# Two table products joined into one VectorE operation, and the whole work list and PSUM pairing written anew, in a kernel of windowed attention beside an S4 convolution

## The chip, the cores and the metric

The kernel runs on one core of one Trainium2 chip. The metric is the device time of one execution in microseconds (us). Before the change three runs took 783.17, 783.67 and 787.14 us; their median, 783.67 us, is the time before. A profile of one execution shows what each engine did: TensorE (PE, with its weight loads as PEld), VectorE (DVE), ScalarE (ACT), GpSimd (POOL) and SyncE (SP, which only issues DMAs here).

## The reference

Two independent layers work on 2048 positions and 576 channels; their outputs stand side by side.

```
A:  qkv = x @ wqkv                       32 heads of 18 channels
    scores = q k^T / sqrt(18), kept where 0 <= i - j < 256
    out_A = softmax(scores) v @ wo
B:  logdA = exp(log_dt) * A              576 channels x 128 complex states
    K[d,l] = Re sum_n C * exp(logdA * l) * exp(log_dt) * B
    y = irfft(rfft(u) * rfft(K)) + u * Dskip
```

## The kernel before, in words

**Layer A.** `proj` makes q, k and v for four blocks of 512 positions. A projection block is 14 matmuls (L204) in three pieces of 5, 5 and 4; its result goes from PSUM through ACT (L450) and DVE (L453) for q and k, or through ACT alone (L442) for v, and is stored to DRAM. The v rows of the first block come earlier, in `vfirst`, from unscaled data (matmuls L398 and L403, ACT copies L405), while the scales of x and w are being found by `amax` (DVE, L192); scaled copies then are made by ACT (L371, L382) and DVE (L372, L383, L385). `smax` finds the largest score of each row: one piece is 8 matmuls (L906 with L914 or L917) and one DVE reduction (L940). `scores` multiplies q and k again (L982, L995), and ACT takes the exponential (L1000); `pv` multiplies by v (L1020); `norm` divides (DVE, POOL and ACT, L1046 to L1063); `wo` applies the output matrix (L204 again, into PSUM pairs).

**Layer B.** The convolution kernel K comes from tables. The 576 channels are 18 quads of 32, each of two half groups of 16 channels: 36 half groups. Per half group: phases on PE (L505), folded into one turn by ACT (L511) and DVE (L514, L515), sines on ACT (L556, L557), a growth factor m on PE with its exponential on ACT (L527, left in PSUM), and on DVE the four products of `t_q` (L601 to L604) that make the table Q. Per quad: factors `mab`, `fa`, sines `tr` (L561, L562), six POOL operations (L567 to L577), and per half group two POOL products (L586) with a DVE sum (L592). From Q and the sums, `t_taps` (64 matmuls, L615) makes the taps of K, ACT moves them (L621), and `t_dft` (L631, L635) transforms a quad. Then come u's first transform (L493), spectra (L718), products (L734, L740), inverse transforms (L752, L815) and output.

**What sets the order.** Every stream of work is a generator, and each step of it (a piece) issues the instructions of one engine or posts an evacuation for later. A string for each of four stages ("front", "tables", "first", "rest") lists the pieces in the order in which they are emitted, one letter a stream, a digit for a posted evacuation: G phases and factors, M growth factor, N sines and the POOL factors, R products and their sum, X taps and transform, P projections, V the first v rows, U u's transform, s row maxima, a scores, v the product with v, w output matrix, and so on. Each engine runs its own instructions in the order of emission; semaphores hold it where data are missing. SP and POOL issue their DMAs in the same order. The streams' pieces are the same whatever the string says; only the order differs.

**PSUM.** Nearly all matmuls outside the projection write into one of three pairs of PSUM banks, `ring0` to `ring2`, each a single buffer. Which pair a step gets is read from a second string, `SLOTS`, a digit per request. A step that gets a pair must wait until the previous user's result has been evacuated.

```
    def slot(self):
        return self.p["ring" + next(self.slots)].tile([128, 2, 512], F32, name="ring")
```

Profile lines of the kernel after stand one lower than those of the kernel before up to `t_q`, where L601 becomes L600, and L603 is gone.

## Time and profile before

| | before |
|---|---|
| runs | 783.17, 783.67, 787.14 us (median 783.67) |
| profiled execution, span | 784.5 us |
| mean granted TensorE clock | 0.963 of full |
| PE busy | 693.0 us (88%) |
| DVE busy | 588.2 us (75%), 779 instructions |
| ACT busy | 534.3 us (68%) |
| POOL busy | 417.3 us (53%) |
| DMA | 150.67 MB |

The span runs from the first to the last instruction of the profiled execution, here 784.5 us, 0.8 us above the median of the runs. Busy time is a sum over the whole program; the stages have different limits, and the time slices of each stage tell which engine stands idle there and for what. The first scaled projection starts at 42.4 us, the first taps at 78.0, the first row maxima at 359.95, the last transform of the tables at 382.98, the last product with v ends at 740.6.

### The profile page before, as it was taken

The page shows a single profiled execution, that of the slowest core. Times are in us where ns is not written, and L with a number is a line of the kernel's source. Part 1 is how long each engine was busy: PE and PEld are TensorE (multiplying, and loading weights), DVE is VectorE, ACT ScalarE, POOL GpSimd, SP SyncE. Part 2 cuts the span into 40 slices and gives each one's busy share as a digit, 9 for nine tenths or more (in the row PEclk, how much of TensorE's full clock was granted, in tenths as well). Part 3 has the DMA queues.
Part 4 walks back from the last instruction along what each step waited for, and adds up shares of the span by engine and source line. Part 5 has one row for each costly group of instructions (what it writes and reads, how often), then busy time and mean ns, then how long its engine had stood idle before and what let it go on. Part 6 is the DMA issues. An engine that isn't in the chain of part 4 may idle for free.

```text
span 784.5 us, 29499 instructions
## 1 busy us (share of the span) xinstructions
PE 693.0 (88%) x12956; PEld 410.8 (52%) x12956; DVE 588.2 (75%) x779; ACT 534.3 (68%) x709; POOL 417.3 (53%) x309
## 2 busy tenths in 40 slices
PE   3786878998989989997789999989989998999997
PEld 2532444565545654665544555544555554557775
DVE  5998789998998897988777888876888586852100
ACT  2369577787887777773458677775877876786622
POOL 2245867987688666866007574451553444546120
PEclk9979799999999999996999999998999999899999
DMA  8998055738247537889578777676866786555786
GB/s 309 342 215 204 7 133 149 159 83 216 51 120 182 133 70 175 230 183 277 113 238 279 247 240 231 207 243 166 245 185 203 240 256 207 170 163 159 205 258 187
DMA packets 215904, 150.67 MB, mean 192 GB/s; under 512 B 103530, under 2 KB 195818, under 8 KB 215520
## 3 DMA queue, kind: packets, MB, share of 16 engines
q1 hardware_dynamic: 214160, 146.28, 66.0%
q0 software_dynamic: 1616, 2.52, 1.1%
q8 instruction: 101, 1.65, 0.8%
q14 instruction: 27, 0.22, 0.1%
HBM read 83.50 MB, written 65.11 MB: 189 GB/s over the span
## 4 chain that ended last, share of the span: by engine, by line
PE 55%; DVE 17%; ACT 15%; issue 6%; DMA 4%; SPq 1%; POOL 0%; ACTq 0%; DVEq 0%
PE po L1020 9%; PE pp L204 9%; PE ring L204 7%; PE ring L906 5%; DVE m L940 5%; PE ring L752 4%; PE ring L982 4%; PE ring L615 4%; PE ring L718 4%; PE ring L505 2%; DMA wraw<-in_wr_dram 2%; DVE amx L192 2%; PE ring L815 2%; ACT raw L1000 2%; DVE wl L372 2%
## 5 line engine op out<-in xcount | busy, mean ns | idle before, releaser
L940 DVE TENSOR_REDUCE m<-ring 128x2 f32<-128x640 f32 (+4 forms) x256 | 190.8, 779 | 66.0 <-PE ring L914 58.2
L586 POOL TENSOR_TENSOR m<-A,tr 128x1024 f32<-128x1024 f32 x72 | 141.5, 1983 | 52.6 <-DVE m L592 43.5
L1000 ACT ACTIVATE P<-ring,esc 128x1024 f32<-128x1024 f32 (+2 forms) x86 | 90.0, 1060 | 37.1 <-PE ring L995 32.7
L1000 ACT ACTIVATE raw<-ring,esc 128x1024 f32<-128x1024 f32 (+2 forms) x74 | 77.2, 1061 | 19.4 <-PE ring L995 18.8
L734 POOL TENSOR_TENSOR t<-X 128x768 f32<-128x768 f32 x24 | 46.7, 1944 | 76.1 <-ACT X L726 75.6
L1063 POOL TENSOR_TENSOR oh<-osb,oh 128x1024 f16<-128x1024 f32 x16 | 34.1, 2133 | 59.5 <-ACT oh L1059 42.9
L914 PE MATMUL ring<-sm,idb 64*64 64x128 bf16 x896 | 56.1, 224 | 3.3 <-issue 3.1
L204 PE MATMUL pp<-xh,wh 128*128 128x512 f16 x180 | 48.1, 397 | 10.0 <-DVE qst L453 5.0
L204 PEld LDWEIGHTS <-wh 128*128 128x128 f16 x324 | 30.7, 99 | 49.1 <-issue 11.7
L615 PE MATMUL ring<-Q,m 128*32 128x64 f32 x2304 | 42.9, 231 | 12.8 <-ACT fa L511 4.1
L1055 POOL TENSOR_TENSOR osb<-osb,T 128x1024 f32<-128x1024 f32 x16 | 38.6, 2410 | 25.8 <-DVE T L1050 23.8
L592 DVE TENSOR_TENSOR m<-m,m 128x1024 f32<-128x1024 f32 x36 | 51.6, 1432 | 0.7 <-POOL m L586 0.6
L615 PEld LDWEIGHTS ring<-Q,m 128*32 128x32 f32 x2304 | 36.9, 117 | 27.2 <-ACT mab L547 5.5
L906 PEld LDWEIGHTS <-raw 54*64 54x64 f16 x704 | 28.6, 108 | 41.1 <-issue 37.7
L740 POOL TENSOR_TENSOR Y<-t,t 128x384 f32<-128x384 f32 x24 | 24.7, 1029 | 46.1 <-DVE t L734 33.8
L906 PE MATMUL ring<-K,raw 54*64 54x320 f16 (+4 forms) x576 | 44.8, 308 | 4.5 <-ACT raw L1000 0.8
L204 PE MATMUL pp<-xh,wl 128*128 128x512 f16 x180 | 48.0, 400 | 0.6 <-DVE wl L372 0.6
L567 POOL TENSOR_TENSOR tr<-tr,mab 128x768 f32<-128x768 f32 x18 | 33.3, 1850 | 28.4 <-ACT tr L562 28.4
L726 ACT ACTIVATE X<-ring 128x768 f32<-128x768 f32 x48 | 36.7, 812 | 14.3 <-PE ring L718 8.1
L995 PE MATMUL ring<-tm,idb 64*64 64x256 bf16 (+2 forms) x640 | 45.0, 257 | 0.0
L982 PEld LDWEIGHTS <-K 55*64 55x64 f16 x1280 | 28.8, 108 | 26.7 <-issue 22.7
L752 PE MATMUL ring<-Y,i 32*64 32x192 f32 x768 | 38.7, 336 | 3.3 <-issue 2.3
(171 smaller groups left out, 1725.1 us busy)
## 6 DMA issues: line engine op xcount, KB each, us to landing
gk<-kst SPq DMA_DIRECT2D x36, 256.0 KB
gx<-ust SPq DMA_DIRECT2D x16, 576.0 KB
xk<-gx SPq DMA_DIRECT2D x24, 384.0 KB
xk<-gk SPq DMA_DIRECT2D x24, 384.0 KB
h<-ho SPq DMA_DIRECT2D x48, 192.0 KB
hp<-h SPq DMA_DIRECT2D x24, 384.0 KB
K<-kz SPq DMA_DIRECT2D x14, 512.0 KB
raw<-qz SPq DMA_DIRECT2D x11, 512.0 KB
```

The source lines that it names most:

```text
L204: self.nc.tensor.matmul(ps, u, v, start=(i == 0), stop=(i == len(ops) - 1))
L586: tt(m[part], A[:, ch, a0:a0 + 8].unsqueeze(3).to_broadcast(sh), tr[:, ch, part, 0:8].unsqueeze(2).to_broadcast(sh), op=OP.mult)
L592: self.nc.vector.tensor_tensor(m[0], m[0], m[1], op=OP.add)
L615: nc.tensor.matmul(kp[32 * st:32 * st + 32, j, :], m[:, ch, 32 * term:32 * term + 32], Q[:, ch, term, :], start=(term == 0), stop=(term == ...
L734: mul(ts[i], X[:, :, :, :192].rearrange("p i s j -> p s i j"), X[:, i, :, 192:].unsqueeze(2).to_broadcast(sh), op=OP.mult)
L752: nc.tensor.matmul(ps[64 * (b % 2):64 * (b % 2) + 64, b // 2, 192 * s:192 * s + 192], self.i1[32 * b:32 * b + 32, t, o:o + 64], Y[32 * b:3 ...
L906: nc.tensor.matmul(ps[z:z + 64, b, :n], d["Q"][rr, 2 * b + pp, 64 * qb:64 * qb + 64], d["K"][rr, 2 * b + pp, k0:k1], start=True, stop=Fals ...
L914: nc.tensor.matmul(out, self.idb[rr], self.sm[rr], start=False, stop=True, skip_group_check=True)
L940: self.nc.vector.tensor_reduce(out, x, axis=AX.X, op=OP.max)
L982: nc.tensor.matmul(ps[z:z + 64, b, off:off + w], d["K"][rr, 2 * b + pp, kc:kc + 64], d["Q"][rr, 2 * b + pp, q0:q0 + w], start=(k == 0), st ...
L1000: nc.scalar.activation(P[:, :, lo:hi], ps[:, :, lo:hi], AF.Exp, scale=self.esc)
L1020: nc.tensor.matmul(po[32 * p:32 * p + 32, z, q0:q0 + w], V[64 * z:64 * z + 64, kb * 76 + 19 * p:kb * 76 + 19 * p + 32], P[p % 2][64 * z:64 ...
```

## The change

Two of the four products of `t_q` read halves of the same sine table f (sine and cosine side by side), multiply by the same 512 values of m, and write neighbouring parts of Q. They become one `tensor_tensor` over 128x1024 elements that reads f with the two halves reversed and m twice by a broadcast. The other two products stay. Over 36 half groups that is 36 DVE instructions fewer, 743 instead of 779. The order strings of all four stages and the string of PSUM pairs are written anew; the pieces in them are otherwise the same ones, and the counts of every other instruction are unchanged, the ACT table loads too.

```diff
 PLAN = {
     "front":
-        "AAAVCACAAAAAVAVVV1CV1CAVAVAAVCAV1ACCVCACCVVV1VV1CVCACBBPABV1CCPV1BV1CPCPP1PVP2PP4CPAPP1PP2BPCP1P4BVP"
-        "CP",
+        "BAAAAAAAAAAVAAACACCCACACVVV1V1VVVV1ACACCCCCCBBBV1CACVVVPAV1BVCCV1VVCV1V1CVVBCPPPPP1",
     "tables":
...
-        "2U2G1RXPP1M1UNP4X1P5PXPGUX1PU1X2PG5X4P5GU4P2MRPU4G2MPPX4G5PP5U2XPG6PG6U4RP6M1PMNXP6GPPMRP4PGNRPRX5P5"
...
-        "5M1P4G6P6RsP5P6NU4sX2P6sU4sRMs2ss2ssX5ss2X4ssZs2s2sss2s2s2Zs2ZX1Ns2ss2sXs2s2X1ss2Rss2XZs2s",
...
+        "XX5P1RP6X2RP4PPMUU2P4P2P1U1XNRX1UP2MUM1U4PU1PPX4U2X4GG1GPMPPP5G2G5GG5G6G6P5XMX1XX4M1U4PX5RRX2MXX1sss"
+        "2s2PRssss2s2ssPs2s2s2ss2PX4X4Nssss2s2Ps2PP5MPM1NX4RRsss2PPP5XX1U4PZs2ZZPMssP6P6s2ss2s2PP5MP5P6RPXPM1"
+        "MRX5XX1X2P4P4Pss6sss2s2X4X4s4ss2sss2s2sss2s2RP5PPPP5sss2Xs2ss2X1XX5X2sss2P6",
...
@@ -598,9 +597,9 @@
         sn, cs = (f[:, i].rearrange("p (c m) -> p c m", m=32) for i in range(2))
         m = self.mg.pop(c)
         Q = self.Q[c] = self.p["Qp"].tile([128, HC, 2, 64], F32, name="Q")
-        tt(Q[:, :, 0, 32:64], cs, m[:, :, 32:64], op=OP.mult)
+        tt(Q[:, :, :, 32:64], f.rearrange("p i (c m) -> p c i m", m=32)[:, :, ::-1],
+           m[:, :, 32:64].unsqueeze(2).to_broadcast([128, HC, 2, 32]), op=OP.mult)
         tt(Q[:, :, 0, 0:32], cs[:, :, ::-1], m[:, :, 0:32], op=OP.mult)
-        tt(Q[:, :, 1, 32:64], sn, m[:, :, 32:64], op=OP.mult)
         nc.vector.scalar_tensor_tensor(Q[:, :, 1, 0:32], sn[:, :, ::-1], -1.0, m[:, :, 0:32],
                                        op0=OP.mult, op1=OP.mult)
```

Three places show what moves.

At the end of the tables, on DVE: before, the last products and sums of the tables stand among the first row maxima (L940), 16 of which come in one row.

```order
L592 TENSOR_TENSOR m_4410<-m_4410,m_4411 128x1024
L601 TENSOR_TENSOR Q<-fr,ring 128x16x32
L602 TENSOR_TENSOR Q<-fr,ring 128x16x32
L603 TENSOR_TENSOR Q<-fr,ring 128x16x32
L604 SCALAR_TENSOR_TENSOR Q<-fr,ring 128x16x32
L940 TENSOR_REDUCE m<-ring 128x2 x16
L926 TENSOR_SCALAR m_4705<-ring 32x128
L647 COPY kst<-ring 128x2x32x8
L940 TENSOR_REDUCE m<-ring 128x2 x2
```

```order
L600 TENSOR_TENSOR Q<-fr,ring 128x32x32
L602 TENSOR_TENSOR Q<-fr,ring 128x16x32
L603 SCALAR_TENSOR_TENSOR Q<-fr,ring 128x16x32
L939 TENSOR_REDUCE m<-ring 128x2 x11
L591 TENSOR_TENSOR m_4300<-m_4300,m_4301 128x1024
L939 TENSOR_REDUCE m<-ring 128x2 x2
L600 TENSOR_TENSOR Q<-fr,ring 128x32x32
L602 TENSOR_TENSOR Q<-fr,ring 128x16x32
L603 SCALAR_TENSOR_TENSOR Q<-fr,ring 128x16x32
L939 TENSOR_REDUCE m<-ring 128x2 x3
```

After, three rows stand where four stood (L600 is the joined product), and the row maxima come in groups of 11, 2 and 3 with a sum and three products between them.

At the same place on ACT: before, the last evacuation of a projection (L442, the v rows `vst`) precedes the last sines of the tables.

```order
L442 ACTIVATE vst_150<-pp,vsc 128x16x18
L511 ACTIVATE fr<-ring 128x512
L527 ACTIVATE ring<-ring 128x1024
L442 ACTIVATE vst_150<-pp,vsc 128x16x18
L556 ACT_TABLE_LOAD
L556 ACTIVATE fr<-fr 128x512
L557 ACTIVATE fr<-fr,halfpi 128x512
L556 ACTIVATE fr<-fr 128x512
L557 ACTIVATE fr<-fr,halfpi 128x512
L561 ACTIVATE tr<-fa 128x32x12
L562 ACTIVATE tr<-fa,halfpi 128x32x12
```

```order
L441 ACTIVATE vst_148<-pp,vsc 128x16x18
L526 ACT_TABLE_LOAD
L526 ACTIVATE ring<-ring 128x1024
L441 ACTIVATE vst_148<-pp,vsc 128x16x18
L620 ACTIVATE Kq<-ring 128x256
L441 ACTIVATE vst_149<-pp,vsc 128x16x18 x2
L526 ACTIVATE ring<-ring 128x1024
L646 COPY kst<-ring 128x2x32x8
L620 ACTIVATE Kq<-ring 128x256
L441 ACTIVATE vst_150<-pp,vsc 128x16x18 x2
L620 ACTIVATE Kq<-ring 128x256
L646 COPY kst<-ring 128x2x32x8
```

After, six evacuations of v rows (L441) stand behind the last sines, among the taps' copies. By the order strings no projection piece stands behind the first row maximum before, and 17 do after.

In the front, on ACT: before, the scaled copies of x and w (L382, L371) stand after all but the last two copies of the first v rows (L405).

```order
L318 ACTIVATE dt<-dt 128x576
L405 ACTIVATE vst_149<-pp 128x16x18
L382 ACTIVATE xh<-raw,xr 128x5x256 x2
L371 ACTIVATE wh<-wraw,wr 128x5x288
L405 ACTIVATE vst_150<-pp 128x16x18 x2
L371 ACTIVATE wh<-wraw,wr 128x5x288 x2
L450 ACTIVATE qst<-pp 128x512
```

```order
L317 ACTIVATE dt<-dt 128x576
L404 ACTIVATE vst_148<-pp 128x16x18
L381 ACTIVATE xh<-raw,xr 128x5x256 x2
L370 ACTIVATE wh<-wraw,wr 128x5x288
L404 ACTIVATE vst_149<-pp 128x16x18
L370 ACTIVATE wh<-wraw,wr 128x5x288 x2
L404 ACTIVATE vst_149<-pp 128x16x18
L370 ACTIVATE wh<-wraw,wr 128x5x288
L404 ACTIVATE vst_150<-pp 128x16x18 x2
L370 ACTIVATE wh<-wraw,wr 128x5x288 x2
L449 ACTIVATE qst<-pp 128x512
```

After, four copies of v rows (L404) stand between and behind the scaled copies, and the first evacuation of a scaled projection (L449) comes behind all six pieces of w.

More of the change, by code (lines that the diff above doesn't have):

```diff
@@ L104 @@
+        "MRX5XX1X2P4P4Pss6sss2s2X4X4s4ss2sss2s2sss2s2RP5PPPP5sss2Xs2ss2X1XX5X2sss2P6",
     "first":
[L105 to L106 removed]
+        "saa1s2ss2s2ss2aass2a1a1vsss6s2ssss2s2sas2s2ss2sss2a1vaaa1s2a1ss2vsaa1s2sasvs2a1X4X4aas2",
     "rest":
[L108 to L109 removed]
```

86 lines of the change are left out of this document (42 added, 44 removed).

## The prediction

> **What bounds the kernel now.** I read the page's totals first, then the time slices cut at the stage borders, then the DVE groups, then the timeline at three places.
>
> ```profile
> span 784.5 us, 29499 instructions
> PE 693.0 (88%) x12956; PEld 410.8 (52%) x12956; DVE 588.2 (75%) x779; ACT 534.3 (68%) x709; POOL 417.3 (53%) x309
> ...
> 20.00:40.00 20.00, 15.96 (x60) 10.06 (x60) 18.68 (x29) 6.52 (x12) 5.39 (x10) 0.93 0.88 330
> 40.00:60.00 20.00, 15.54 (x62) 6.48 (x63) 19.92 (x17) 13.26 (x16) 7.60 (x4) 0.82 0.96 219
> 60.00:100.00 40.00, 30.15 (x247) 14.57 (x247) 32.55 (x47) 30.96 (x49) 29.41 (x25) 0.83 0.46 109
> 100.00:220.00 120.00, 106.97 (x1537) 62.15 (x1536) 108.27 (x147) 95.91 (x152) 92.17 (x70) 0.99 0.54 128
> 220.00:340.00 120.00, 111.40 (x1492) 66.35 (x1490) 105.50 (x146) 90.92 (x147) 87.82 (x69) 1.00 0.64 158
> 340.00:358.00 18.00, 15.30 (x263) 10.83 (x267) 14.66 (x19) 14.79 (x26) 12.30 (x11) 1.00 0.84 193
> 358.00:370.00 12.00, 9.28 (x220) 6.74 (x213) 10.65 (x19) 2.24 (x6) 8.32 (x10) 0.50 0.97 293
> 370.00:382.00 12.00, 9.07 (x239) 6.87 (x235) 9.89 (x17) 5.71 (x7) 3.89 (x2) 0.79 0.56 122
> 382.00:420.00 38.00, 31.56 (x894) 17.84 (x882) 26.32 (x43) 22.21 (x29) 7.55 (x6) 1.00 0.71 213
> 420.00:740.00 320.00, 301.40 (x7651) 175.94 (x7648) 228.31 (x292) 234.88 (x253) 151.95 (x96) 0.98 0.71 214
> 740.00:784.50 44.50, 39.79 (x329) 28.66 (x312) 2.85 (x3) 12.46 (x16) 6.60 (x3) 1.00 0.70 218
> ```
>
> Columns of the slices: length, busy us of PE, PEld, DVE, ACT and POOL with instructions, granted clock, DMA share, GB/s. PE is busy 693.0 of 784.5 us, so 91.5 us of idling and what a low clock stretches is all that a new order can win, since the same matmuls run. After 420 PE is full (301.4 of 320): little to win. From 20 to 60 DVE is full (38.6 of 40). From 100 to 340 PE (218.4 of 240) and DVE (213.8 of 240) are both near their limit, each waiting now and then for the other. From 358 to 382 both idle a little (PE 5.65 of 24, DVE 3.46) and the clock stands at 0.50 for half of it. From 382 to 420 PE idles 6.44 us.
>
> The costs on DVE, by groups (columns: instructions, shapes, count, busy us, mean ns, idle before and for what):
>
> ```profile
> L940 DVE TENSOR_REDUCE m<-ring 128x2 f32<-128x640 f32 x224 | 176.4, 821 | 60.0 <-PE ring L914 58.2
> L592 DVE TENSOR_TENSOR m<-m,m 128x1024 f32<-128x1024 f32 x36 | 51.6, 1432 | 0.7 <-POOL m L586 0.6
> L515 DVE TENSOR_SCALAR fr<-fr 128x512 int32<-128x512 int32 x36 | 35.7, 992 | 1.2
> L601 DVE TENSOR_TENSOR Q<-fr,ring 128x512 f32<-128x512 f32 x36 | 24.5, 680 | 7.6 <-ACT ring L527 4.9 <-PE ring L615 2.0 <-ACT fr L557 0.7
> L302 DVE TENSOR_TENSOR rre<-nA_re,hre 96x768 f32<-96x768 f32 x1 | 0.9, 945 | 0.0
> ```
>
> **Part 1, the joined product.** One half group in the timeline of DVE (start, duration), and one sum of 1024 elements beside it:
>
> ```profile
> 206.25 0.68 DVE L601 TENSOR_TENSOR Q<-fr,ring 128x512 f32<-128x512 f32 x1
> ...
> 207.44 0.68 DVE L603 TENSOR_TENSOR Q<-fr,ring 128x512 f32<-128x512 f32 x1
> ...
> 213.19 1.21 DVE L592 TENSOR_TENSOR m<-m,m 128x1024 f32<-128x1024 f32 x1
> 214.32 0.68 DVE L647 COPY kst<-ring 128x512 f32<-128x512 f32 x1
> ```
>
> The products overlap: 0.68 us long, but two of them take 207.44 - 206.25 = 1.19 us of DVE's time. The trace has no product of 1024 elements with an operand in PSUM. The nearest row, L592, has both operands in SBUF and in this undisturbed case takes 214.32 - 213.19 = 1.13 us from start to start. So the join saves 1.19 - 1.13 = 0.06 us, 36 times: 2.3 us. Upper bound: the joined product reads m once and costs no more than one of 512 (0.60): 36 x 0.59 = 21 us. Lower bound: it takes the mean of L592, 1.43, which is stretched by POOL's products beside it: 36 x (1.19 - 1.43) = -8.6 us. I take 2.3, since the elements written are as many as before and the undisturbed row is of that size; an operand in PSUM speaks against the stretched one, as L601 shows (680 ns mean, against 0.68 undisturbed).
>
> [...]
>
> What of the 2.3 us reaches the end? DVE is a bound from 100 to 340, where 28 of the 36 lie, but it shares that with PE. I count half here, 1.2 us.
>
> **Part 2, the front.** The first scaled projection waits for DVE's maxima, then ACT's copies:
>
> ```profile
> 10.75 3.15 DVE L192 TENSOR_REDUCE amx<-wraw 128x1 f32<-128x2880 f32 x1 [4.17 <-DMA wraw<-in_wr_dram]
> ...
> 35.15 1.48 DVE L192 TENSOR_REDUCE amx<-raw 128x1 f32<-128x1280 f32 x1
> ...
> 37.16 0.56 POOL L252 DMA_DIRECT2D c_ca<-in_c_ca_dram  x1
> ...
> 38.08 2.61 ACT L382 ACTIVATE xh<-raw,xr 128x1280 f16<-128x1280 f32 x2 [2.56 <-DVE xr L188]
> ...
> 40.60 1.48 ACT L371 ACTIVATE wh<-wraw,wr 128x1440 f16<-128x1440 f32 x1
> ...
> 42.42 2.29 PE L204 MATMUL pp<-xh,wh 128*128 128x512 f16 x5 [2.76 <-ACT vst L405]
> ...
> 78.01 1.29 PE L615 MATMUL ring<-Q,m 128*32 128x64 f32 x40 [4.12 <-ACT fa L511]
> ```
>
> In the new order the four operations of L302 (945 ns each, 3.8 us) come ahead of the first maximum, into DVE's 4.17 us gap before 10.75, where they cost nothing; before, they stand between maxima. Against that, POOL issues the four table constants (0.74 MB by their shapes) at the start, and not from 37.16 on, after the scales: at the 330 GB/s of the slice 20 to 40 that is 2.2 us ahead of the last blocks of x, if DMA has no slack (it is 0.88 busy there, so 0 to 2.2). At the worst of that 1.6 us remain, which I take. The copies of v (L405) move behind ACT's scaled copies, so that the first projection starts some 4 to 5 us later (two copies of x, 2.61 us, and one of w, 1.48, stand ahead of the buffers it needs). I price this at nothing: before the first taps fewer projection pieces stand in the front (5 against 12), and DVE, not PE, carries the path to the taps at 78; PE only waits there (4.12 us). Without that cover it costs the 5 us, and part 3 has the pieces to fill less. Bounds for the front: -5 to +4.
>
> **Part 3, the end of the tables.** Before, nothing but row maxima and the last three half groups are left for PE:
>
> ```profile
> 357.42 1.57 PE L615 MATMUL ring<-Q,m 128*32 128x64 f32 x64 [1.10 <-DVE kst L647]
> ...
> 359.95 0.27 PE L906 MATMUL ring<-raw 54*64 54x64 f16 x4 [0.95 <-ACT kst L647]
> ...
> 361.51 7.83 DVE L940 TENSOR_REDUCE m<-ring 128x2 f32<-128x128 f32 x14
> ...
> 369.94 0.38 ACT L621 ACTIVATE Kq<-ring 128x256 f32<-128x256 f32 x1 [9.76 <-PE ring L615]
> ```
>
> Each maximum is a matmul group, a wait, and a DVE reduction of up to 0.82 us, through three PSUM pairs: DVE sets the pace (14 in 7.83 us), the matmuls are too thin, the clock falls, and the taps behind them come late (ACT waits 9.76 us for them). In the new order 17 projection pieces stand among these maxima, which before are all done by then. Such a piece is five matmuls of 128x288:
>
> ```profile
> L204 PE MATMUL pp<-wh,xh 128*128 128x288 f16 x120 | 18.7, 286 | 1.9 <-ACT vst L442 0.9 <-DVE qst L453 0.9
> 740.54 0.79 PE L204 MATMUL ring<-woh,oh 128*128 128x288 f16 x5
> 741.16 0.78 PE L204 MATMUL ring<-wol,oh 128*128 128x288 f16 x5
> ```
>
> From start to start five such take 0.62 us (the other rows of the output matrix), so 17 pieces are about 10 us of PE work that needs no DVE (L442 evacuates them on ACT, which has only 2.24 us to do in 358 to 370). They leave the stage from 100 to 340, where PE runs at 91%, and go where PE idles 5.65 us and is slow. What they win cannot exceed what DVE has free, since DVE's work up to the last transform of the tables stays: 3.46 us between 358 and 382 and 3.34 between 340 and 358. I take the first, 3.5 us, and 1.0 for the 0.50 clock: in those 12 us 9.28 are busy, at full clock at most half, 4.6, would be saved, but DVE paces most of that. Bounds: 0 (the idle time only moves) to 5.65 + 4.6 = 10.
>
> **Part 4, behind the tables.** From 382 to 420 PE idles 6.44 us and DVE 11.68, on chains of maximum, score and exponential that wait for each other. The new order starts more maxima early: the tables hold 29 of them where 17 stood, and the "first" stage is 18 pieces shorter. Twelve maxima are 12 x 0.82 = 9.8 us of DVE work moved ahead; they fill holes there, and here PE's wait shrinks. I take a quarter of the 6.44, 1.6 us; bounds -3 to 5. From 420 to 740 PE has 18.6 us idle; the same pieces in another order give no row that prices them, so 0, with -6 to +6 (a third either way).
>
> At the end one row of SP's queue, the load of the last output block:
>
> ```profile
> 760.65 0.93 SPq L1129 DMA_DIRECT2D oh<-od  x1
> ```
>
> After the last product with v, the final normalization, its DMA round trip and the last output block stay a chain; in SP's order an output of the convolution now comes ahead of that block's loads. That is one DMA issue, which takes up to 0.93 us here (this row); half of it, -0.4.
>
> **The sum.** 1.2 + 1.6 + 3.5 + 1.0 + 1.6 + 0 - 0.4 = 8.5 us, which I round to 8, from 784.5 to 776.5 us of the profile. The median of the runs shown, 783.67, lies 0.8 below that execution, so the prediction is 775.7 us.
>
> **The rivals.** (1) *The idle time only moves.* For it: up to 382 DVE has the same work but for 2.3 us, and both PE and DVE are near full from 100 to 340, so that pieces pulled out of the tables leave holes there. Then only the join and half of the front count: 1.2 + 0.8 = 2 us, 781.7. Against it: the projection pieces are independent of DVE's chain in the tail.
>
> (2) *Slower: POOL's products stretch DVE.* The fold in the view of its line (least, median, most ns):
>
> ```profile
> L515 DVE TENSOR_SCALAR fr<-fr x36: 426/854/2252, 60.2 to 355.0; 128x512 int32<-128x512 int32 x36
> ```
>
> DVE operations with both sides in SBUF are long whenever POOL works beside them: L592 means 1432 ns against 1.21 undisturbed, L515 992 where the fastest takes 426, so 36 x (0.22 + 0.56) = 28 us are lost now. In the new order M, X and G pieces come in clusters; if the folds and sums fall behind POOL's products a third more often, 9 us are added to DVE, which carries the tables; with the late first projection (5 us, part 2) taken as hidden this gives 784.5 + 9 - 2.3 (join) - 0.8, about 790. It decides as soon as the stretch grows by more than the 8 us won, some 30%. Against it: POOL's work is unchanged and the products stay 72.
>
> (3) *The clock stays up.* If the 17 pieces keep PE above the point where the clock falls, all of the 4.6 us in 358 to 370 comes back, not 1.0: 772. For it: the slices before 358 and after 382, with denser PE work, stand at 1.00.
>
> [...]
>
> **How the numbers follow.** My forecast, 773 to 779.5, has 0.45; the clock case, 767 to 773, 0.15; idle time that only moves, 780 to 786, 0.22; the slower case, 787.6 to 796, 0.18. A measurement of this kernel tells no less than about 0.5%, 3.9 us, from no change: faster means under 779.8, slower over 787.6. So faster 0.60, same 0.22, slower 0.18. The range from 767 to 787.6 leaves out the slower case and a few hundredths below; the likeliest case's own range is 773 to 779.5.
>
> **What would show it.** The join: a group of 36 at 128x1024 near 1.2 us mean, 1.13 from start to start where nothing waits; 1.4 would show the lower bound. The front: first taps at about 76.4, not 78.0; over 80 shows the late copies of v. The tail: projection matmuls among the first maxima, the last transform of the tables at about 376, not 383, and clock above 0.50 there. Rival 1: the last transform at 381 or later with PE idle higher in 100 to 340. Rival 2: L591 (the sum) over 1.5 us and L514 (the fold) over 1.1 us mean, DVE's busy time over 595 us. The prediction is wrong if the stage after 420, which I took as even, gains or loses more than 6 us.

## The result

The changed kernel is slower: 814.15 us median (810.06 to 815.98) against 783.42 for the kernel before on the same chip, a ratio of 1.038 with the interval [1.033, 1.043]. The profiled execution took 812.7 us where the one of before took 784.5. The forecast was 775.7, with the range ending at 787.6. A few executions of a kernel run more than 1.5% above its fastest one; the medians and ratios below leave these out.

The totals of the page after:

```profile
span 812.7 us, 29455 instructions
...
PE 697.1 (86%) x12956; PEld 410.1 (50%) x12956; DVE 602.1 (74%) x743; ACT 534.7 (66%) x709; POOL 424.9 (52%) x309
```

PE does the same 12956 matmuls in nearly the same busy time (697.1 against 693.0): 24.1 of the 28.2 us are idling. DVE has 36 instructions fewer and yet is busy 13.9 us longer.

The slices of the prediction, cut at the same times (length, busy us of PE, PEld, DVE, ACT, POOL with instructions, granted clock, DMA share, GB/s):

```profile
20.00:40.00 20.00, 12.49 (x45) 8.24 (x44) 15.17 (x14) 2.83 (x6) 1.04 (x2) 0.90 1.01 387
...
100.00:220.00 120.00, 104.72 (x1445) 60.98 (x1444) 107.54 (x125) 91.04 (x143) 90.65 (x70) 0.96 0.55 134
220.00:340.00 120.00, 104.62 (x1417) 60.31 (x1421) 106.77 (x124) 88.79 (x144) 89.53 (x70) 0.99 0.56 136
...
358.00:370.00 12.00, 10.00 (x266) 6.86 (x264) 11.68 (x20) 8.41 (x15) 5.29 (x4) 1.00 0.73 166
...
420.00:740.00 320.00, 292.14 (x7495) 166.99 (x7495) 233.23 (x296) 228.75 (x249) 151.41 (x97) 0.98 0.68 207
```

Three losses and one gain stand in these rows. From 20 to 40 DVE is no longer full (15.17 of 20 where it was 18.68): it waits, beside a full DMA (1.01, 0.88 before). From 100 to 340 PE does less in the same time (209.3 us of 240, 218.4 before) while DVE is as full as it was (214.3, 213.8 before). From 420 to 740 PE has lost 9.3 us. And the thin stage from 358 to 370 stands at full clock with DVE at 11.68 of 12: this is the one place where the change does what was forecast.

Fixed times shift as the kernels part, so the rest of this text cuts by landmarks in the work instead: the first taps matmul, the 15th and the 18th (last) transform of the tables, the first spectrum, the end of the last product with v. Length of each stage in us, by the start of these matmuls in the traces; e1 is the kernel before with the joined product alone, whose execution is closest to the medians of the old order. (A run's time is 1.7 to 1.8 us above its span, 814.44 for 812.7 and in e1 780.72 for 778.9; so the profiled execution of before, 784.5, took some 786.2 us, 2.6 above its median, where the prediction set span and median side by side and took 0.8.)

```
                                   before     e1   after
start to first taps                  78.0   77.8    82.6
tables, to the 15th transform       256.5  253.6   264.1
end of the tables, 15th to 18th      48.5   49.7    44.1
18th transform to first spectrum     23.6   23.5    29.4
first spectrum to last v            334.1  329.4   340.8
last v to the end                    43.9   44.9    51.7
all                                 784.5  778.9   812.7
```

Against e1 the change loses 4.8 in the front, 10.4 in the tables, wins 5.7 at their end, and then loses 5.9, 11.4 and 6.8. The work between two landmarks isn't quite the same, since the order moves matmuls past them. PE's idle time in each stage, and the matmuls that start in it (e1 has the matmuls of before):

```
                                 idle, us: before     e1   after     matmuls: before  after
start to first taps                          28.2   28.0    31.8                 188    180
tables, to the 15th transform                25.2   24.9    34.5                3170   3136
end of the tables, 15th to 18th               8.6    8.5     4.3                 789    815
18th transform to first spectrum              4.8    4.5     6.1                 490    586
first spectrum to last v                     20.0   18.3    28.2                8016   7944
last v to the end                             4.7    5.5    10.7                 303    295
all                                          91.5   89.7   115.6               12956  12956
```

So most of the 5.9 us behind the 18th transform is work: 96 matmuls more stand ahead of the first spectrum, and 72 fewer behind it. Over the end of the tables the granted clock is 1.00 where it was 0.82, and DVE is busy 42.4 us of 44.1 where it was 40.6 of 48.5. Five stages lose and one wins: no single wait does it, so the experiments take them apart.

### The profile page after: what moved, and what is told of

Same layout as the page of the kernel before. It is cut to its first block, busy times and chain, and to the rows that moved or that the text cites. A ratio compares the mean times of both kernels' runs of the same rounds, so it can differ in the third digit from the quotient of the medians.

```text
span 812.7 us, 29455 instructions
## 1 busy us (share of the span) xinstructions
PE 697.1 (86%) x12956; PEld 410.1 (50%) x12956; DVE 602.1 (74%) x743; ACT 534.7 (66%) x709; POOL 424.9 (52%) x309
## 3 DMA queue, kind: packets, MB, share of 16 engines
q8 instruction: 101, 1.65, 0.9%
## 4 chain that ended last, share of the span: by engine, by line
PE 38%; DVE 26%; DMA 16%; SPq 7%; issue 6%; ACT 6%; POOL 0%; ACTq 0%; DVEq 0%; POOLq 0%
PE po L1019 6%; PE pp L203 6%; PE ring L203 6%; DVE m L939 4%; PE ring L905 4%; DMA hp<-h 4%; DMA K<-kz 4%; PE ring L981 3%; DVE m L591 3%; DMA wraw<-in_wr_dram 3%; DVE Q L600 3%; PE ring L751 3%; PE ring L717 2%; PE ring L492 2%; DVE Q L602 2%
## 5 line engine op out<-in xcount | busy, mean ns | idle before, releaser
L585 POOL TENSOR_TENSOR m<-A,tr 128x1024 f32<-128x1024 f32 x72 | 144.0, 2017 | 60.2 <-DVE m L591 51.5
L591 DVE TENSOR_TENSOR m<-m,m 128x1024 f32<-128x1024 f32 x36 | 60.8, 1689 | 4.1 <-POOL m L585 4.1
L739 POOL TENSOR_TENSOR Y<-t,t 128x384 f32<-128x384 f32 x24 | 24.1, 1003 | 59.5 <-DVE t L733 36.7
L614 PE MATMUL ring<-Q,m 128*32 128x64 f32 x2304 | 39.9, 222 | 14.1 <-DVE m L591 4.9
L600 DVE TENSOR_TENSOR Q<-fr,ring 128x1024 f32<-128x1024 f32 x36 | 43.6, 1212 | 6.6 <-ACT ring L526 6.4
L614 PEld LDWEIGHTS ring<-Q,m 128*32 128x32 f32 x2304 | 34.5, 111 | 25.9 <-issue 6.3
L397 PE MATMUL pp<-wraw,raw 128*128 128x288 f32 x64 | 23.1, 528 | 26.9 <-DMA raw<-in_xr_dram 16.5
```

The source lines that it names most:

```text
L585: tt(m[part], A[:, ch, a0:a0 + 8].unsqueeze(3).to_broadcast(sh), tr[:, ch, part, 0:8].unsqueeze(2).to_broadcast(sh), op=OP.mult)
L591: self.nc.vector.tensor_tensor(m[0], m[0], m[1], op=OP.add)
L600: tt(Q[:, :, :, 32:64], f.rearrange("p i (c m) -> p c i m", m=32)[:, :, ::-1], m[:, :, 32:64].unsqueeze(2).to_broadcast([128, HC, 2, 32]), ...
L614: nc.tensor.matmul(kp[32 * st:32 * st + 32, j, :], m[:, ch, 32 * term:32 * term + 32], Q[:, ch, term, :], start=(term == 0), stop=(term == ...
```

## Experiments

Theory A at the start was that the joined product is harmless and the order costs the time; the rival, that the join costs it.

### The join alone, and the order alone (e1, e2)

e1 is the kernel before with this edit, e2 the changed kernel without it:

```diff
-        tt(Q[:, :, 0, 32:64], cs, m[:, :, 32:64], op=OP.mult)
+        tt(Q[:, :, :, 32:64], f.rearrange("p i (c m) -> p c i m", m=32)[:, :, ::-1],
+           m[:, :, 32:64].unsqueeze(2).to_broadcast([128, HC, 2, 32]), op=OP.mult)
...
-        tt(Q[:, :, 1, 32:64], sn, m[:, :, 32:64], op=OP.mult)
```

> The kernel before with the joined product alone, order and PSUM pairs as they were. Theory A (the loss is all in the order; the join is worth its rows, 0.06 us of DVE 36 times, and DVE shares the limit with PE): 781 to 784 us. Rival B (the join itself costs: one operation of 1.2 us holds DVE longer where others wait behind it, or reads PSUM slowly): over 787 us.

> The kernel after with the four separate products, so the new order alone. Theory A: the whole loss stays and the join's 1 to 2 us are missing: 815 to 818 us. Rival B (the join is the cause): under 795 us.

e1 measured 782.69, ratio 1.003 [0.999, 1.006]; e2 measured 813.99, ratio 1.042 [1.034, 1.049]. The join moves the time by nothing that can be measured, and the order with its pairs carries the whole loss. In e1 the joined product has this row among the groups of DVE:

```profile
L601 DVE TENSOR_TENSOR Q<-fr,ring 128x1024 f32<-128x1024 f32 x36 | 43.7, 1214 | 6.2 <-ACT ring L527 4.9 <-ACT fr L557 0.7 <-PE ring L615 0.4
```

### Which stages (e3, e4)

e3 takes the old order through the stages "tables" and "first" and the new one for "rest"; e4 the reverse. Both have the joined product, and each part its own PSUM pairs. Only the tables of order change:

```diff
 PLAN = {
-    "front": (new)    "tables": (new)    "first": (new)
+    "front": (old)    "tables": (old)    "first": (old)
     "rest": (new)
```

> Joined product; the pieces up to the end of the tables in the old order, all that is left in the new order. In the trace of after, the last transform of the tables ends 7.7 us late, the first spectrum starts 13.6 us late, the last product with v ends 20 us late and the program 28 us. Theory A (each stretch loses its own share): 783 - 1 + 28 - 10 to 13 = 797 to 800 us. Rival B (the later stages only inherit the late start of the tables): 782 to 786 us. Rival C (only the later stages lose): 808 us and more.

> Joined product; the pieces up to the end of the tables in the new order, all that is left in the old order. Theory A: 783 + 8 to 13 = 791 to 796 us. Rival B (the loss starts in the tables and grows by itself): 808 us and more. Rival C (only the later stages lose): 782 to 786 us.

e3: 806.22, ratio 1.032 [1.025, 1.039]. e4: 792.93, ratio 1.015 [1.008, 1.023]. The new order of the rest costs 23 to 25 us, that of front and tables 9 to 11, together 32 to 36, a little more than the 31 to be explained. By the landmarks e3 takes 342.7 us from the first spectrum to the last v and 50.6 to the end; e4 takes 328.0 and 44.6, as the old order does. The stretch from the 18th transform to the first spectrum is 28.3 us in e3, behind the old tables, and 25.8 in e4, behind the new ones: most of its growth, too, comes with the order of the rest.

### The front (e5, e9)

e5 takes the old front and the new order behind it. e9 keeps the new front and moves one step of POOL's queue, the issue of the four constants of the tables, from ahead of everything to behind the scales:

```diff
     "front":
-        "BAAAAAAAAAAVAAACACCCACACVVV1V1VVVV1ACACCCCCCBBBV1CACVVVPAV1B...
+        "AAAAAAAAAAVAAACACCCACACVVV1V1VVVV1ACACCCCCCBBBBV1CACVVVPAV1B...
```

> The kernel after with the first stage in the old order (its pieces up to the first twelve projection pieces), all the rest in the new one. In the trace of after the first taps start at 82.6 us, not 78.0, and the first projection at 53.3, not 42.4. Theory A (the front's delay is carried to the end): first taps at 78, total 808 to 810 us. Rival B (it is absorbed, since DVE sets the pace of the tables): 813 us and more.

> The kernel after with one piece of the front put back: GpSimd issues the four table constants after the scales, as before the change. In the trace of after DVE's first maximum waits until 14.56 us for its weights, not 10.75, and the scale of x is known 4.0 us later. Theory A (the constants ahead delay x and w by their own time, and that is the front's loss): scale of x at 38 us, first taps 3 to 4 us earlier than in after, total 809 to 811 us. Rival B (the copies of the first v rows behind the scaled copies are the front's loss): first taps within 1 us of after, total 813 us and more.

e5: 809.57, ratio 1.038 [1.032, 1.045]; e9: 807.92, ratio 1.035 [1.027, 1.043]. These medians are 4.6 and 6.2 us below the changed kernel's, but the kernel before, run beside them, was faster too (781.0 and 782.6), and the ratios can't be told from the 1.038 [1.033, 1.043] of the change: the gain is seen in the traces, not in the totals. There the first taps start at 77.8 (e5) and 78.5 (e9) for 82.6, and the last transform at 385.9 and 385.6 for 390.7. So the constants ahead are 4.1 us, nearly all, of the front's loss. The timeline, first of the changed kernel, then of e9 (start, duration, idle before and for what):

```profile
14.56 3.15 DVE L191 TENSOR_REDUCE amx<-wraw 128x1 f32<-128x2880 f32 x1 [4.22 <-DMA wraw<-in_wr_dram]
...
42.13 2.62 ACT L381 ACTIVATE xh<-raw,xr 128x1280 f16<-128x1280 f32 x2 [3.48 <-DVE xr L187]
```

```profile
10.51 3.15 DVE L190 TENSOR_REDUCE amx<-wraw 128x1 f32<-128x2880 f32 x1 [0.47 <-DMA wraw<-in_wr_dram]
...
19.97 3.15 DVE L190 TENSOR_REDUCE amx<-wraw 128x1 f32<-128x2880 f32 x1 [3.51 <-DMA wraw<-in_wr_dram]
...
38.24 2.62 ACT L380 ACTIVATE xh<-raw,xr 128x1280 f16<-128x1280 f32 x2 [2.56 <-DVE xr L186]
49.04 1.24 PE L202 MATMUL pp<-xh,wh 128*128 128x512 f16 x5 [0.49 <-ACT vst L403]
```

The constants put the first block of w 3.8 us later on DVE (14.56, 10.75 before), and every maximum behind it. That is more than their bytes: from 7 to 15 us, with DMA full in all three (1.02, 1.04 and 1.01), it moves 366 GB/s before, 302 in the changed kernel and 360 in e9. Why the rate falls is not shown. e9 also shows two things that were only argued. The four operations of L302, moved out from between the maxima, win nothing: the maxima that they made room for now wait 3.51 us for the next block of w and ACT's scaled copies start at 38.24, 38.08 before. And the late copies of v cost next to nothing: the first scaled projection starts at 49.04 instead of 42.42, and yet the first taps come at 78.5, 78.0 before.

### The tables: DVE beside POOL (e7, e8, e11, e12)

The tables lose 10 us in front of their end. DVE does the same work there, but some of its operations on SBUF take longer. The groups in the changed kernel, and one line of it by its view (least, median and most ns; who waited):

```profile
L591 DVE TENSOR_TENSOR m<-m,m 128x1024 f32<-128x1024 f32 x36 | 60.8, 1689 | 4.1 <-POOL m L585 4.1
...
L514 DVE TENSOR_SCALAR fr<-fr 128x512 int32<-128x512 int32 x36 | 31.8, 883 | 1.2
...
L600 DVE TENSOR_TENSOR Q<-fr,ring 128x1024 f32<-128x1024 f32 x36 | 43.6, 1212 | 6.6 <-ACT ring L526 6.4
...
L384 DVE SCALAR_TENSOR_TENSOR xh<-raw,xr,xh 64x256 f16<-64x256 f32 x8 | 8.7, 1082 | 0.1
```

```profile
L591 DVE TENSOR_TENSOR m<-m,m x36: 1205/1238/3008, 81.2 to 387.8; 128x1024 f32<-128x1024 f32 x36
...
  POOL m L585: 51.5, 18
```

The sums went from 51.6 to 60.8 us, the small pieces of x (L384, 485 ns mean before) to more than twice their time. The folds did not grow (31.8, 35.7 before). Half of the sums take their undisturbed 1.2 us; the others up to 3.0. One such place (DVE, then POOL, then PE):

```profile
107.72 2.97 DVE L382 SCALAR_TENSOR_TENSOR xl<-raw,xr,xh 128x1024 f16<-128x1024 f32 x1
110.71 2.08 DVE L384 SCALAR_TENSOR_TENSOR xh<-raw,xr,xh 64x256 f16<-64x256 f32 x1
112.80 1.28 DVE L382 SCALAR_TENSOR_TENSOR xl<-raw,xr,xh 128x1024 f16<-128x1024 f32 x1
114.10 0.48 DVE L384 SCALAR_TENSOR_TENSOR xh<-raw,xr,xh 64x256 f16<-64x256 f32 x1
...
105.56 6.95 POOL L585 TENSOR_TENSOR m<-A,tr 128x1024 f32<-128x1024 f32 x3
...
114.64 0.59 PE L203 MATMUL pp<-xh,wh 128*128 128x512 f16 x1 [4.27 <-DVE xh L384]
```

The same two operations take 2.97 and 2.08 us while POOL's products run (up to 112.5) and 1.28 and 0.48 just behind them, and PE waits 4.27 us for the result. In all, PE waits 7.2 us for these pieces of x between 100 and 340 us (2.1 before, 2.7 in e1), about half of the idle time that the tables have more. The joined product, with an operand in PSUM, takes 1202 to 1223 ns in all its 36 places: at 93.17, for one, 1.21 us beside POOL's products (91.02 to 96.98), where the sum at 100.12, with both operands in SBUF, takes 2.83 us beside L566 and L571 (100.05 to 103.44). Why POOL stretches the one and not the other is not shown.

A first idea was that the sums meet POOL's products more often in the new order, and that the other order of the two products would pull them apart:

```diff
-        for part, a0 in ((0, 4), (1, 0)):
+        for part, a0 in ((1, 0), (0, 4)):
```

> The kernel after with GpSimd's two products of a half group in the other order: the one whose result has a single buffer comes first. GpSimd then can't start the next half group's products until DVE has made the sum, so sum and product no longer run side by side. Theory A (the sums, 1.69 us mean in after against 1.43 before, are stretched by GpSimd's products beside them, and that holds up the tables): sums at 1.2 to 1.35 us mean, tables' end 6 to 10 us earlier, total 804 to 809 us. Rival B (DVE's stretch is not on the path, or what GpSimd loses by waiting comes back as late products): 813 us and more.

> The kernel before with the joined product and GpSimd's two products in the other order. Theory A: sums from 1.45 to 1.2 to 1.35 us mean, some 5 us of DVE: 777 to 781 us. Rival B: 783 us and more.

e7 (in the new order): 817.97, ratio 1.048, the sums at 64.8 us: not shortened, so the idea falls. e8 (in the old order, with the join): 786.10, ratio 1.007 [1.003, 1.011], the sums at 57.7, the folds 10 us less than in e1, and POOL waits 67.9 us for the sums where it waited 42.5 in e1; the last transform comes at 388.3, 381.2 in e1. DVE as a whole was stretched less and the tables still came later: POOL's own lateness is a part of the path.

The overlaps, counted from the starts and ends in the traces, name another partner: the sums lie beside POOL's growth factor and the first product behind it (L566 and L571) for 26 us in the new order and 14 in the old. e11 and e12 shorten the growth factor, in the new order and in the old one with the join. It is applied to 8 of the 32 channels of a group and left out for the other 24:

```diff
-        tt(tr, tr, self.mab.pop(q).unsqueeze(2).to_broadcast([128, GC, 2, 12]), op=OP.mult)
+        tt(tr[:, 0:8], tr[:, 0:8], self.mab.pop(q)[:, 0:8].unsqueeze(2).to_broadcast([128, 8, 2, 12]), op=OP.mult)
```

> The kernel after with GpSimd's product of sines and factors made for 8 of 32 channels only (the growth of the others is left out). In the trace of after this operation (1.85 us) and the one behind it run beside DVE's sums for 26 us in all, in before for 14. Theory A (that stretch of DVE holds up the tables): sums' mean from 1.69 to under 1.45 us, tables' end 5 us and more earlier, and more than in the same edit of the kernel before. Rival B (DVE's stretch is hidden): tables' end within 2 us.

> The kernel before with the joined product and the same edit: GpSimd's product of sines and factors for 8 of 32 channels only (the growth of the others is left out). Theory A: sums' mean from 1.46 to about 1.35 us, tables' end 1 to 3 us earlier, total 778 to 782 us. Rival B: no change, 781 to 784 us.

In the new order: 809.66, ratio 1.033 [1.024, 1.043], which alone can't be told from the changed kernel's; the sums fall to 49.6 us and the last transform comes 4.2 us earlier (386.5 for 390.7), less than the 5 expected. Of these 4.2 us, 1.8 are won before the first taps (80.8 for 82.6) and 1.0 between them and the 15th transform. PE still waits 6.9 us for the pieces of x. In the old order: 782.78, ratio 1.000 [0.996, 1.004], although its sums fall as well, to 46.6, and the last transform comes at 383.0, 381.2 in e1. By these traces the same POOL work lies on the path in the new order and beside it in the old. The edit shortens POOL's own work together with the stretch of DVE beside it, so it doesn't show which of the two the path feels. The groups, in e11 and in e12:

```profile
L591 DVE TENSOR_TENSOR m<-m,m 128x1024 f32<-128x1024 f32 x36 | 49.6, 1377 | 4.1 <-POOL m L585 4.1
```

```profile
L592 DVE TENSOR_TENSOR m<-m,m 128x1024 f32<-128x1024 f32 x36 | 46.6, 1296 | 0.1
```

### Do the parts add up? (e17, e18)

e17 is e4 with the constants late as in e9; e18 is e17 with the growth factor short as in e11 (left out for 24 of 32 channels).

> New order through the tables and the first stage with the constants of the tables issued late, after the scales (as in e9), and the old order and pairs of the rest (as in e4, 792.9). Theory A (the losses of front, tables and rest add up): e4's 792.9 less the 4 to 6 us that the late constants gave in e9, 787 to 789; 782 to 783 for the kernel before leaves 5 us on the tables. Theory B (the losses hide each other): less than 2 us are won, over 791, or the whole is, under 785.

> e17 with POOL's growth factor applied to 8 of the 32 channels of a group alone (left out for the other 24), which takes POOL's work from beside DVE's sums. Theory A (what is left of the tables' loss is the stretch of DVE beside POOL): 3 to 5 us less than e17, 782 to 785, level with the kernel before. Theory B (it is the order itself, late copies and pairs): within 1.5 us of e17.

e17: 787.72, ratio 1.009 [1.006, 1.013]; e18: 784.73, ratio 1.004 [1.000, 1.008]. e17 lies where the sum of the parts put it. e18 wins 3.0 us more, at the lower end of the 3 to 5 expected and with intervals that overlap; what stays above the kernel before is at the edge of what can be told. In e18's profile the last transform comes at 379.8, 386.1 in e17. So the constants ahead, the order of the rest and, for about 3 us, POOL's growth factor (by its own length or by what it does to DVE) account for the loss; none of these kernels is faster than the kernel before.

### The end (e6)

In the changed kernel the last outputs of the convolution and the last output blocks stand in a chain on SP. PE, from 780 on, and SP's issues of the loads that it waits for:

```profile
780.44 0.87 PE L814 MATMUL ring<-hp,i 128*64 128x384 f32 x4 [1.12 <-DMA hp<-h]
784.37 1.55 PE L814 MATMUL ring<-hp,i 128*64 128x384 f32 x4 [3.06 <-DMA hp<-h]
785.85 1.38 PE L203 MATMUL ring<-woh,oh 128*128 128x288 f16 x5
...
780.69 0.42 SPq L803 DMA_DIRECT2D hp<-h  x1
...
785.39 0.38 SPq L1128 DMA_DIRECT2D oh<-od  x1
```

The load for 784.37 is issued at 780.69, behind eight loads of output blocks, and the loads of the next block follow at 785.39, behind stores. e6 takes the old order from the 15th normalization on (normalization, output matmuls and everything beside them):

> The kernel after with its last pieces, from the normalization of the item before the last, in the old order: the last two convolution outputs then stand behind the third output block on TensorE, and the load of the last block's second half ahead of fewer stores on SyncE. In the trace of after the last block starts 29 us late where the last product with v ends 20 us late. Theory A (TensorE stands in order behind convolution outputs whose loads SyncE issues late): 806 to 808 us. Rival B (the last normalization's own chain sets the end): 813 us and more.

e6: 810.24, ratio 1.033 [1.020, 1.046], span 808.5: neither theory's time, and not to be told from the changed kernel by the ratio. By the landmarks it takes 49.1 us from the last v to the end, 51.7 in the changed kernel, and so wins 2.6 of the 6.8 to 7.8 us lost here. PE waits 4.2 us for the loads of convolution outputs in the changed kernel and no longer in e6; it waits 3.6 us for ACT's evacuations and 2.4 for output blocks instead. The chain of loads is a part of the loss here; the rest is not taken apart.

### The rest: pairs, or code (e10, e13 to e16)

From the first spectrum to the last v the new order takes 341 us, the old one 329 to 334. First suspect: the pairs. e10 has the order of the changed kernel, its pairs given anew by one rule (the pair whose last user's release stands earliest in the order); 222 of the 727 uses then follow another piece.

```diff
 SLOTS = (
-    "0120102020102101020102021021022012210021210202120101...
+    (each use takes the pair that is released first in the order)
```

> The kernel after with the PSUM pairs named by one plain rule: each request gets the pair whose last evacuation stands furthest back in the order (222 of 727 requests then follow another user). Theory A (the loss is in the order of pieces, not in the pairs): within 4 us of after, 810 to 818 us. Rival B (the new pairs make matmuls wait for evacuations): under 806 us.

e10: 834.32, ratio 1.070 [1.061, 1.079]. Neither theory had that: pairs alone can cost 20 us. PE's waits in that stage of e10:

```profile
PE ring L980 <- DVE m L938: 6.8, 14, 0.9
PE ring L904 <- ACT P L998: 6.2, 10, 1.2
PE ring L904 <- DVE m L938: 4.7, 9, 1.3
```

It doesn't acquit or convict the pairs of the changed kernel. The waits do more: the gaps of PE over 0.1 us that end with an operation of ACT or DVE, as evacuations are, sum to 13.4 us behind the tables before, 15.2 in the changed kernel and 44.3 in e10. At most about 2 us of the loss are these.

Second suspect: code. In the list of PE's waits from 421 to 741 us the largest entries have no releaser ("issue"), before and after:

```profile
PE ring L914 <- issue: 3.1, 5, 1.2
PE ring L982 <- issue: 2.7, 3, 1.7
PE ring L752 <- issue: 2.3, 1, 2.3
```

```profile
PE ring L981 <- issue: 3.5, 3, 1.4
PE po L1019 <- issue: 2.7, 2, 1.8
PE ring L913 <- issue: 2.6, 4, 1.1
PE ring L905 <- issue: 2.6, 4, 1.0
PE ring L751 <- issue: 2.2, 2, 1.2
```

One of them cuts a product with v in two, where nothing is waited for; the page lists a queue of the kind "instruction" whose packets (code, below) fit:

```profile
572.32 0.24 PE L1019 MATMUL po<-raw,V 64*32 64x64 f32 x1
574.32 0.35 PE L1019 MATMUL po<-raw,V 64*32 64x64 f32 x9 [1.76 <-issue]
```

```profile
q8 instruction: 101, 1.65, 0.9%
```

A packet of q8 starts at 571.89 and takes 1.06 us; PE goes on 2.43 us after its start. That distance returns: in this stage of the changed kernel all eleven gaps over 0.6 us that end with no releaser end 2.3 to 2.9 us after such a packet began. 101 packets of 16 KB are 1.65 MB, one for about 257 of PE's 25,912 instructions in the mean, and 52 to 432 of them start between one packet and the next. That these packets are PE's code, in blocks of 256 instructions (as the expectations below have it), is an estimate from the counts. PE's gaps over 0.15 us from the first spectrum to the last v, and those of them that end 2.0 to 3.2 us after a packet of code:

```
                 all gaps   behind code   other
old order  before    17.3       10.0       7.2
           e1        15.6        8.0       7.6
           e4        15.5        8.1       7.5
           e17       15.5        9.5       6.0
new order  after     25.4       17.5       7.9
           e3        26.6       13.1      13.6
           e9        24.3       12.3      12.0
```

In the changed kernel 7.5 of the 8 us more lie behind code. e13 to e16 put 32 or 64 small matmuls at the very start, where PE has nothing to do for 16 us, in the new order (e13, e14) and in the old one with the join (e15, e16); by that estimate they shift the blocks of code against the work.

```diff
+            warm = self.p["ring0"].tile([128, 2, 512], F32, name="ring")
+            for j in range(64):
+                nc.tensor.matmul(warm[:, 0, :32], self.ones[:, 128 * (j % 2):128 * (j % 2) + 128], self.ones[:, :32],
+                                 start=True, stop=True)
             self.known, self.conv_n = False, 0
```

> Changed kernel with 32 small matmuls ahead of everything, on PE, which has nothing to do before 16 us; they shift the 256-instruction blocks of PE's code by a quarter block, all else is as it was. In the trace the gaps of PE that end 2.0 to 3.2 us after the start of a code packet of queue q8 sum to 17.5 us from the first spectrum to the last product with v in the changed kernel, against 8 to 9 in the kernels with the old order of the rest. Theory A (a property of the order): the sum stays at 12 to 20 us and the time at 808 to 820. Theory B (luck of where the blocks end): the sum changes freely, here to anything between 6 and 20, and the time follows it by as much.

> The same with 64 small matmuls, half a block of code. Theory A: 12 to 20 us of gaps behind code packets, 808 to 820. Theory B: at least one of the shifted kernels of the new order falls to 9 us or less, its time to 807 or less.

> The old order with the joined product (782.7, 8 us of gaps behind code packets) with the same 32 small matmuls ahead. Theory A: 4 to 10 us of gaps, 780 to 786. Theory B: as free as in the new order, so that one of the two shifted kernels of the old order reaches 12 us or more, and 787 or more.

> The old order with the joined product and 64 small matmuls ahead. Theory A: 4 to 10 us of gaps behind code packets, 780 to 786. Theory B: 12 us or more in one of the two, and 787 or more.

```
                 time     ratio [95%]             all gaps   behind code   other
new order  e13  812.60   1.043 [1.037, 1.048]       23.4        9.8        13.6
           e14  813.77   1.042 [1.038, 1.047]       28.4       12.2        16.2
old order  e15  784.22   1.005 [1.002, 1.009]       16.5        8.6         7.9
           e16  786.76   1.008 [1.004, 1.012]       17.1       10.0         7.1
```

Each theory is half right. As the second said, the gaps behind code change with the matmuls put ahead: 17.5, 9.8 and 12.2 in three kernels of the same order. As the first said, the time does not follow: 812.6 and 813.8, 814.2 in the changed kernel. Where code takes less, other waits take more, and the sum of all gaps stays with the order: 23.4 to 28.4 in the new one, 15.5 to 17.3 in the old. In e14, for one, PE waits for loads of K instead, and for DVE:

```profile
PE ring L905 <- DMA K<-kz: 4.4, 3, 2.9
PE ring L913 <- issue: 3.4, 2, 2.0
PE ring L981 <- DVE m L939: 3.1, 9, 0.5
PE ring L905 <- DVE m L939: 2.7, 8, 1.1
```

Over all profiles the waits of this stage part by the order. In the ten kernels with the new order of the rest and its pairs (the changed one, e2, e3, e5 to e7, e9, e11, e13, e14) PE waits (gaps over 0.1 us) 7.5 to 16.2 us with no releaser and 3.2 to 6.7 for loads; in the nine with the old one (before, e1, e4, e8, e12, e15 to e18) it is 2.7 to 9.5 and 0 to 2.5. Its waits for ACT (3.6 to 6.6 and 4.6 to 6.0) and for DVE (4.3 to 7.8 and 3.0 to 5.1) differ less.

So the matmuls put ahead change in which waits the loss shows, and the gaps behind code are not its cause. What the order does to lose these 8 to 10 us of idling stays open. Two things differ that could: by the strings of the order, PE gets two pieces of row maxima in a row 54 times (35 before) and single ones 100 times (146 before), and the loads on SP come 13 times in bunches of three or more without a piece for PE between them (twice before). Neither was tried by itself.

## Why the prediction was wrong, step by step

**What bounds the kernel.** Read rightly: PE's idling is what an order can change, and 24.1 of the 28.2 us are idling. "After 420 PE is full: little to win" overlooked that there was much to lose, and this is where the larger part went.

**Part 1, the join.** The mechanism was right. The joined product takes 1212 ns in the mean, and in the timeline of the changed kernel 105.30 - 104.17 = 1.13 us from start to start, as its row L592 had promised:

```profile
104.17 1.21 DVE L600 TENSOR_TENSOR Q<-fr,ring 128x1024 f32<-128x1024 f32 x1
105.30 0.68 DVE L602 TENSOR_TENSOR Q<-fr,ring 128x512 f32<-128x512 f32 x1
```

Of the 1.2 us forecast nothing can be seen in e1 (0.3% above the kernel before, interval -0.1 to +0.6%). DVE's busy time does fall by the 2.3 us of the sum, from 588.2 to 585.9 in e1; that it doesn't reach the end fits a stage with two full engines.

**Part 2, the front (+1.6 forecast, -4.6 measured, at the end of the bounds of -5 to +4).** Two terms failed. The constants were priced at 0 to 2.2 us by dividing bytes by the mean rate; they cost 3.8, since they go ahead of the first block of w, on which everything waits, and DMA, full behind them, moved 302 GB/s for 366. The 3.8 us won by the moved L302 were counted from DVE's rows alone; e9 shows that DVE then waits 3.51 us for the next block of w. The slice from 20 to 40 had DMA at 0.88: the stage was bound by loads nearly as much as by DVE. The third step, the late copies of v at nothing, held: in e9 the first projection starts 6.6 us later, not 4 to 5, and the first taps only 0.5. The sign "over 80 shows the late copies of v" misled: the taps at 82.6 came from the constants.

**Part 3, the end of the tables (+4.5 forecast).** Right in size, and the signs of the mechanism are there: 48.5 to 44.1 us from the 15th to the 18th transform, PE's idle time 8.6 to 4.3 us, the clock over this stage 1.00 for 0.82. That the projection pieces did it is argued and not shown, for no run moves them alone. Nor is it shown at what load of PE the clock falls: it is 0.50 with PE busy 9.28 of 12 us (358 to 370, before) and 0.90 with 12.49 of 20 (20 to 40, after).

**Part 4, behind the tables (+1.6 forecast).** The wait that more maxima ahead should have shortened did not shrink: PE idles 6.1 us from the last transform to the first spectrum, 4.8 before. The stretch as a whole grew from 23.6 to 29.4 us, most of it by the 96 matmuls that moved into it.

**The tables in front of their end (nothing forecast, 7.6 to 10.4 us lost).** Here the second rival was right in part: the sums went over its mark of 1.5 us (1.69) and DVE over 595 (602.1). It was wrong on the folds (883 ns, under the mark of 1.1; at 90.23 one takes 0.43 us beside POOL's L575 and L576, so "whenever" was too wide) and on the partner: "POOL's work is unchanged" spoke against it, and the sums grew with the placing of an unchanged operation: they lie beside the growth factor and what follows it for 26 us where it was 14, and fall to 49.6 us when it is shortened (e11). e11 puts 4.2 us up to the last transform on that operation, 1.8 of them in the front; PE's longer wait for the x pieces, as at 114.64, is 4 to 5 us. What is left of it is not taken apart. The first rival's sign came too: the last transform at 390.7, later than 381, with PE idle 30.7 us of the 240 from 100 to 340 where it was 21.6. Whether the pieces pulled to the end left these holes, no run tells. That the second rival's 790 lies near the 792.93 of e4 is in part luck: it took the front's loss as hidden, and e4 has 5 us there.

**From 420 on (0 forecast, -6 to +6).** The failing step: "the same pieces in another order give no row that prices them, so 0". The stage lost 6.8 to 11.4 us (340.8 for 334.1 and 329.4), above the bound and with 72 matmuls fewer in it; PE idles there 28.2 us for 20.0 and 18.3, in waits with no releaser and for loads. The time from the last v lost 7 to 8 more where -0.4 was forecast. The latter was there to be read in the order: an issue on SP was priced by its 0.93 us, not by the landing that PE waits for behind it (3.06 us) nor by the stores ahead. The former could not be priced from a row, and its cause stays open, but its bounds were drawn around nothing, as if a tuned row of waits were as easily better as worse.

**The chances.** The slower case held 0.18 with one mechanism in one stage. With five stages re-ordered, the losses of each could add up, and did; the forecast let the gains add up and took the losses as rivals of each other.

## What to carry to other kernels

Where a new order touches all stages, price each stage for loss as well as for gain: the stage after 420, with PE busy 301.4 of 320 us, had little to win and lost 6.8 to 11.4, and losses in separate stages add (e3, e4 and e17 show it). Compare stages by landmarks in the work, and count what moved past them, before a stage is called slower. A small transfer ahead of the first large load can cost more than its bytes: here 3.8 us, beside a full DMA (1.04), where 0 to 2.2 were priced. An operation moved out of a busy engine's way wins nothing if the next input is not there earlier (in e9 DVE waits 3.51 us for it). And a wait that stands large in one profile is a cause only if the time follows when it is removed: the gaps behind code fell from 17.5 to 9.8 us and the time moved by no more than 2.

## What the runs showed that was not expected

- PE stood still behind packets of code. About 63 packets of 16 KB come from the first spectrum to the last v, and 10 to 25 of them have a gap that ends 2.0 to 3.2 us after the packet starts, 8 to 17.5 us together in the kernels of the two tables above. That is 42 to 69% of all gaps; windows of 1.2 us behind 63 packets would hold some 22% of them by chance. What holds PE there is not shown.
- Pairs by a plausible rule, in the same order, cost 20 us (e10), about as much as the whole new order of the rest.
- POOL beside DVE made a DVE operation of 0.48 us take 2.08, and sums of 1.2 us up to 3.0; taking away three quarters of one POOL operation brought the sums from 60.8 to 49.6 us, and the last transform of the tables 4.2 us forward in the new order, but not in the old one, where it came 1.8 us later.
